# A transformer block on one core: the opening of the attention stage put in another order

## The chip, the core and the metric

The kernel runs on one core of a Trainium2 chip. Its engines are TensorE (PE, matrix products; PEld is its loading of the stationary operand), VectorE (DVE), ScalarE (ACT), GpSimd (POOL) and SyncE (SP, which mostly issues transfers). Each engine works through its own list of instructions strictly in order, and semaphores hold an instruction back until what it reads is there. Operands lie in SBUF, products are accumulated in PSUM, and both are laid out as 128 partitions by so many columns. The metric is the device time of one execution in microseconds (us); lower is better. Before the change the median of three runs is 546.14 us (545.97 to 547.85).

## The reference

The block has a linear attention half (A) and a token-mixing MLP half (B), 2048 tokens by 1024 channels, weights and inputs in bf16:

```python
h  = x + A(layernorm(x), wqkv, wo)
h2 = h + B(layernorm(h), w1, b1, w2, b2)

# A, 32 heads of 32 channels
q, k, v = split(x @ wqkv)
phi = lambda t: where(t > 0, t + 1, exp(t)) + 1e-6
pq, pk = phi(q), phi(k)
kv  = einsum("bhsd,bhse->bhde", pk, v);  z = einsum("bhsd->bhd", pk)
o   = einsum("bhqd,bhde->bhqe", pq, kv) / (einsum("bhqd,bhd->bhq", pq, z)[..., None] + 1e-6)
A   = o @ wo

# B, over the token axis, after a layernorm of its own
u = gelu(einsum("bsd,sf->bdf", layernorm(x), w1) + b1)
B = transpose(einsum("bdf,fs->bds", u, w2) + b2)
```

`A_x` is [1, 2048, 1024], `A_wqkv` [1024, 3072], `w1` [2048, 3584], `w2` [3584, 2048].

## The kernel before

The 2048 tokens are cut into 16 tiles of 128 (`x_sb`, one row of 1024 channels per partition). Each tile is normalised: `bn_stats` over each half of 512 columns and `bn_aggr` on DVE give mean and variance (`ln_chunks`, L1098 and L1101), two small ACT instructions turn the variance into 1/sqrt (Ln, then Exp; L1104 and L1105; below "the scales"), and DVE subtracts and multiplies (L1108, `xn`). The result is turned so that channels lie on partitions (`xnT`): for tiles 0 to 3 by PE transposes into PSUM (`transpose_half`, L1444) and copies back by ACT (L1454, L1484, L1487), for later tiles by a transposing DMA issued by SP (L1125).

From `xnT` PE makes keys, values and queries. For tiles 0 and 1 this is done plainly, in units of 128 tokens by 512 output columns and eight matmuls, one for each block of 128 channels (`proj_mm`, L1129): `k_unit(i, c)` for the keys of tile i and column half c, `proj_unit(i, 2 + c)` for the values. Each matmul reads a slice of the weights `wkv`, which SP loads column half by column half: c = 0 in three pieces, c = 1 in two pieces of four channel blocks (L1428), c = 2 and 3 (the values) in one piece each (L1432), then the query weights `wq_sb`. The loads of the token tiles stand between them in the same queue: tile 2 ahead of the first piece of c = 1, tile 3 ahead of its second, tiles 4 and 5 behind the first half of `wq_sb`. Tile 0 comes as two halves of columns, one by SP and one by ACT's queue, and tile 1 by ACT's queue (`load_x`). While nothing has landed, PE does products on a tile of zeros (`warm_up`).

From tile 2 on, keys, values and queries are made in `Run`s of two tiles by the seven products of the Strassen-Winograd scheme. Each run's seven products `p1` to `p7` need sums of the weight blocks (`w_sums`, L1187: four for the keys, then four for the values) and of the token blocks (`x_sums`, L1202), all made by DVE. `run_step(n, prev)` interleaves a run with the last two products of the run before: `p1` of n, `p3` and `p4` of prev, then `p6`, `p2`, `p5`, `p7` of n. `p7` and `p3` end with a DVE addition (`add`, L1307 for keys and queries, L1284 for values) that reads PSUM, and `p4` writes on into the bank that the addition of `p7` has read, so PE's `p4` waits for that addition. The order of the runs is K(1), V(1), K(2), V(2), ..., with query runs between the later ones and three (r1, r2, r3) behind; the digit is the pair of tiles.

The feature map `phi` is made in parts (`phi_parts`): `act` writes exp into `e_sb` (L200) and, unless `lean`, relu into `r_sb` (L202), both on ACT; `dve` clips and shifts `e_sb` in place (L205, below "clip") and adds the two (L209, or L207 when lean; below "join"). A key or query run makes four such maps, named by token half and column half: `dve11`, `dve21`, `dve12`, `dve22`. In `run_step` `dve22` follows `p3`, and `dve21` follows `p6`; on DVE nothing lies between them, so the order there is clip, join, clip, join.

`pin` keeps the instructions it is given in program order on their engine; `ln_stats(i)` is the statistics of tile i, `ln_finish(i)` its scales, normalisation and transposing DMA. In the main loop (L1620 to L1698) `after6`, `after5`, `finish` and `after7` say behind which product of which run these stand. The four `k_unit`s, the transposes of tiles 2 and 3 and their DVE and ACT work stand in the order written out by hand at L1490 to L1545. Two `memset`s of `zz` (L1681, L1682), which need nothing, are placed by the scheduler between DVE's first statistics. The MLP half after 183 us is not touched.

Of the kernel before, what the change touches and what calls it, by code (L numbers as in the profile page):

```python
# [10 lines left out]
P = 128  # L11
# [26 lines left out]
def kernel(  # L38
# [156 lines left out]
    def phi_parts(dst, src, n, pool, view=lambda t: t, lean=False):  # L195
        e_sb = pool.tile([P, n], BF16, tag="phi_e", name="e_sb")
        r_sb = None if lean else pool.tile([P, n], BF16, tag="phi_r", name="r_sb")

        def act():
            pin(nc.scalar.activation(e_sb[:], src, ACT.Exp))  # L200
            if not lean:
                pin(nc.scalar.activation(r_sb[:], src, ACT.Relu))  # L202

        def dve():
            pin(nc.vector.tensor_scalar(e_sb[:], e_sb[:], 1.0, PHI_EPS, ALU.min, ALU.add))  # L205
            if lean:
                pin(nc.vector.scalar_tensor_tensor(dst, view(src), 0.0, view(e_sb[:]), ALU.max, ALU.add))  # L207
            else:
                pin(nc.vector.tensor_tensor(dst, view(e_sb[:]), view(r_sb[:]), ALU.add))  # L209

        return act, dve

    def phi_evac(dst, src, n, pool):
        for part in phi_parts(dst, src, n, pool):
            part()

    sactx = ctx.enter_context(ExitStack())
    mctx = ctx.enter_context(ExitStack())
# [792 lines left out]
    with ExitStack() as actx:  # L1011
# [33 lines left out]
        with ExitStack() as a1:  # L1045
# [5 lines left out]
            vaugs = [a1w.tile([P, ND * HB, DH + 1], BF16, name=f"vaug{t}") for t in range(NVA)]  # L1051
            for t in range(NVA):
                nc.vector.memset(vaugs[t][:, :, DH:DH + 1], 1.0)

            def heads(t, c):
                return t[:, c * JB * HB:(c + 1) * JB * HB, 0:DH]
# [22 lines left out]
            def load_x(i, halves=False, q=nc.sync):  # L1079
                x_sb = xload.tile([P, D], BF16, name="x_sb")  # L1080
                if halves:
                    nc.sync.dma_start(x_sb[:, 0:CW], x[i * P:(i + 1) * P, 0:CW])
                    pin(nc.scalar.dma_start(x_sb[:, CW:D], x[i * P:(i + 1) * P, CW:D]))
                else:
                    dma = q.dma_start(x_sb[:], x[i * P:(i + 1) * P, :])
                    if q is not nc.sync:
                        pin(dma)
                return x_sb
# [115 lines left out]
            class Run:  # L1204
# [56 lines left out]
                def dve11(self):  # L1261
                    pass

                def dve21(self):
                    pass

                def dve12(self):
                    pass

                def dve22(self):  # L1270
                    pass

            class VRun(Run):
                def __init__(self, q):
# [13 lines left out]
            class KRun(Run):  # L1288
# [25 lines left out]
                    self.phi[1, 1][0]()  # L1314

                def dve11(self):
                    self.phi[0, 0][1]()

                def dve21(self):
                    self.phi[1, 0][1]()  # L1320

                def dve12(self):
                    self.phi[0, 1][1]()

                def dve22(self):
                    self.phi[1, 1][1]()

            class QRun(KRun):
                lean = True
# [51 lines left out]
            def run_step(n, prev, after6=None, after5=None, after7=None, fill=None, after3=None):  # L1381
                if n is not None:
                    n.p1()
                else:
                    fill()
                prev.late22()
                prev.p3()
                if after3 is not None:
                    after3()
                prev.dve22()  # L1390
                prev.p4()
                if n is not None:
                    n.p6()
                prev.dve21()
                if after6 is not None:
                    after6()
                if n is not None:
                    n.p2()
                    n.p5()
                prev.late12()  # L1400
                if n is not None:
                    n.dve11()
                behind = QRun in (type(n), type(prev)) or type(n) is VRun
                if not behind:
# [24 lines left out]
                if k0 == 0:  # L1429
                    xs[3] = load_x(3)  # L1430
            for c in range(2, 2 * NDC):
                nc.sync.dma_start(wkv[:, :, c * CW:(c + 1) * CW], wqkv_v[:, :, D + c * CW:D + (c + 1) * CW])  # L1432
            for c in range(NDC):
                nc.sync.dma_start(wq_sb[:, :, c * CW:(c + 1) * CW], wqkv_v[:, :, c * CW:(c + 1) * CW])
                if c == 0:
# [11 lines left out]
            def stats(i):  # L1447
                for op in ln[i][3]():
                    pin(op)
# [21 lines left out]
                    phis[key][0]()  # L1471

            def phi_dve(*keys):
                for key in keys:
                    phis[key][1]()

            def k_unit(i, c):
                phis[i, c] = k_parts(i, c)
# [18 lines left out]
            stats(0)  # L1497
            pin(ln[1][1](0))
            norm_halves(0)
            transpose_first(0, 0, 0)  # L1500
            pin(ln[1][1](1))
            pin(ln[1][2]())
            stats(1)
            k_parts(0, 0, range(0, 6))
            norm_halves(1)
            transpose_first(1, 6, ND)
            ln_stats(2)
            stats(2)
            k_unit(1, 0)
            norm_halves(2)  # L1510
            phi_act((0, 0))
            k_unit(0, 1)
            phi_act((1, 0))
            transpose_in(2)
            ln_stats(3)
            stats(3)
            phi_dve((0, 0))
            w_sums(kmov, slice(0, 1))
            norm_halves(3)
            phi_dve((1, 0))  # L1520
            phi_act((0, 1))
            k_unit(1, 1)
            transpose_in(3)
            phi_dve((0, 1))
            x_sums(1)
# [93 lines left out]
            for q in range(1, NVP):  # L1619
# [6 lines left out]
                for n in runs:  # L1626
                    kind = type(n).__name__[0]
                    i = {"K": 2 * q + 3, "V": 2 * q + 4}.get(kind, NS)
                    if q == 5 and kind == "Q":
                        i = NS - 1 if n.half == 1 else NS  # L1630
                    elif q == 6 and kind == "K":
                        i = NS

                    def after6():
                        if i < NS:
                            ln_stats(i)

                    def after5():
                        if kind == "K" and q % 2 == 1:
                            kv_block(q - 2)  # L1640
                        if kind != "V" and (kind, q) != ("K", 2):
                            finish()

                    def finish():
                        if i < NS:
                            ln_finish(i)
                            load_next(i + 2)

                    def after7():
                        if (kind, q) == ("K", 2):  # L1650
                            finish()
                        if kind == "V":
                            if q != 5 and q + 1 < NVP:
                                x_sums(q + 1, slice(0, 2))
                            prev.dve12()
                            finish()
                            if q != 5 and q + 1 < NVP:
                                x_sums(q + 1, slice(2, 4))
                        if q == 5 and kind == "Q" and n.half == 1:
                            x_sums(q + 1, slice(0, 3))  # L1660
                        if kind == "K" and q in q_sums:
                            w_sums(qmov, q_sums[q])
                        for m, a in moved_at.get((kind, q, getattr(n, "half", 0)), ()):
                            q_moved(m, a)
                        for x in late_sums.get((kind, q), ()):
                            x_sums(x[0], x[1], late_parts)
                        if (kind, q, getattr(n, "half", 0)) in fill_at:
                            q_fill()
                        if n is runs[-1] and q == 7:
                            kv_accum(NS - 2)  # L1670
                            kv_accum(NS - 1)

                    def after3():
                        if q == 6 and type(prev) is QRun:
                            x_sums(q, slice(3, 4))

                    run_step(n, prev, after6, after5, after7, after3=after3)
                    prev = n
            first_parts, first_home = sums_home(NSC - 1)
            r1, r2, r3 = (QRun(u, half, home, late_mov) for u, half, home in ((1, 0, late_home), (1, 1, late_home), (0, 1, first_home)))  # L1680
            nc.vector.memset(zz[:, :, 0:3 * HB], 0.0)  # L1681
            nc.vector.memset(zz[:, :, 3 * HB:], float(S))  # L1682

            turned = kvbd[:].rearrange("p (b a) (r e) -> p a b r e", b=HB, e=DH)
            sums_v = kv_ps[:, :, 0:DH].rearrange("p (b a) e -> p a b e", b=HB)
# [147 lines left out]
        with ExitStack() as a3:  # L1833
# [137 lines left out]
            fill[1]()  # L1971
# [3 lines left out]
            r3.dve21()  # L1975
            last[1][0]()
            for f in (r3.dve22, r3.dve12, last[0][1], last[1][1]):
                f()
# [315 lines left out]
```

## Time and profile before

| | |
|---|---|
| median of the runs | 546.14 us (545.97, 546.14, 547.85) |
| profiled execution | 545.59 us, its span 543.7 us |
| PE busy | 538.0 us (99%) |
| DVE busy | 471.3 us (87%) |
| ACT busy | 315.2 us (58%) |
| chain that ended last | PE 95%, DMA 2%, ACT 1%, DVE 1% |
| first transposes on PE | 6.21 us |
| first product of K(1) on PE | 23.48 us |

The span is the time from the first to the last instruction of one execution as the profiler recorded it; 1.9 us of that execution's device time lies around it. A row of the timeline gives start, length, engine, line, operation, tiles, shapes and count, and in brackets the engine's idle time just before and what ended it. PE's matmuls overlap, so its true pace is read from the starts: sixteen matmuls of 512 columns in a row take 3.45 us in the chain of waits, 0.216 us each.

### The profile page before, as it was taken

To read this page: it belongs to the slowest core of one execution; us is meant where nothing else is said; L and a number is where in the kernel's file an instruction comes from. 1 tells how busy PE (TensorE), PEld (TensorE's weight loads), DVE (VectorE), ACT (ScalarE), POOL (GpSimd) and SP (SyncE) were. 2 spreads that over 40 slices of the span, in tenths; PEclk is the share of its full clock that TensorE was granted. 3 is DMA by queue.
4 is the path that set the end of the run, shared out by engine and by line. 5 is a ranking of instruction groups with operands and counts; after the bars stand their busy time and mean duration, and the time that the engine had idled before them with its cause. 6 is when DMAs were issued, how large, how long until landed. Compare 5 with 4: busy or idle time off the path is not lost.

```text
span 543.7 us, 10593 instructions
## 1 busy us (share of the span) xinstructions
PE 538.0 (99%) x4046; PEld 339.4 (62%) x4058; DVE 471.3 (87%) x934; ACT 315.2 (58%) x672; POOL 73.1 (13%) x78
## 2 busy tenths in 40 slices
PE   8999999999999999999999999999999999999997
PEld 3444456656874444456777777776455667867865
DVE  7999897867798678899999989999898899979877
ACT  5678778767787788666667677675210413312320
POOL 1000000000002450021123112120002103103111
PEclk9999999999999999999999999999999999999999
DMA  8944321203339999137375856756697759399344
GB/s 293 326 79 98 88 69 21 40 1 93 82 94 238 220 277 320 74 40 155 40 151 65 160 83 127 156 68 147 173 299 196 208 133 243 53 304 223 80 128 74
DMA packets 105378, 77.76 MB, mean 143 GB/s; under 512 B 16482, under 2 KB 97904, under 8 KB 105328
## 3 DMA queue, kind: packets, MB, share of 16 engines
q1 hardware_dynamic: 85536, 64.32, 42.3%
q0 software_dynamic: 19360, 12.34, 17.4%
q8 instruction: 31, 0.51, 0.4%
q10 hardware_dynamic: 432, 0.44, 0.2%
q14 instruction: 19, 0.16, 0.1%
HBM read 62.27 MB, written 11.67 MB: 136 GB/s over the span
## 4 chain that ended last, share of the span: by engine, by line
PE 95%; DMA 2%; ACT 1%; DVE 1%; issue 0%; SPq 0%; DVEq 0%
PE psI L253 32%; PE psC L253 20%; PE psA L253 5%; PE psB L253 5%; PE psC L1213 5%; PE acc_t L253 4%; PE psB L1213 4%; PE psA L1213 4%; PE psE L1213 2%; PE psC L1347 2%; PE psA L1347 2%; PE psB L1347 2%; PE psF L253 2%; DMA wkv<-in_A_wqkv_dram 2%; PE acc_t L1129 1%; PE psE L253 1%
## 5 line engine op out<-in xcount | busy, mean ns | idle before, releaser
L253 PEld LDWEIGHTS <-is 128*128 128x128 f16 x900 | 87.9, 98 | 32.5 <-issue 0.3
L253 PEld LDWEIGHTS <-wq 128*128 128x128 bf16 (+1 forms) x694 | 67.9, 98 | 36.7
L253 PEld LDWEIGHTS <-sa 128*128 128x128 f16 x467 | 45.6, 98 | 13.9 <-issue 1.0
L253 PEld LDWEIGHTS <-pqT 128*128 128x128 bf16 x256 | 24.7, 98 | 30.6 <-issue 1.3
L526 POOL DMA_DIRECT2D out_dram<-wq x28 | 24.3, 937 | 143.4 <-ACT wq L529 96.8
L253 PE MATMUL psC<-gs,wq 128*128 128x512 f16 x168 | 40.8, 379 | 0.0
L1894 POOL DMA_DIRECT2D h_bf<-in_A_x_dram x18 | 16.1, 1079 | 183.2 <-ACT h_bf L253 182.9
L1213 PEld LDWEIGHTS <-xs 128*128 128x128 f16 x224 | 21.6, 98 | 24.3 <-DVE xs L1202 0.3
L253 PE MATMUL psI<-hi,is 128*128 128x256 f16 x240 | 36.0, 272 | 0.0
L253 PE MATMUL psC<-hT,wq 128*128 128x512 f16 x112 | 34.1, 379 | 0.0
L253 PE MATMUL psC<-hT,sa 128*128 128x512 f16 x112 | 32.0, 379 | 0.0
L253 ACT COPY psI<-psI 128x256 f32<-128x256 f32 x60 | 21.5, 358 | 15.8 <-PE psI L253 13.4
L1213 PE MATMUL psA<-wkv,xnT 128*128 128x512 bf16 x104 | 27.8, 379 | 0.4
L1213 PEld LDWEIGHTS <-xnT 128*128 128x128 bf16 x168 | 16.3, 98 | 19.0 <-issue 0.2
L253 PE MATMUL psI<-gi,is 128*128 128x256 f16 x210 | 27.8, 273 | 0.0
L168 POOL DMA_DIRECT2D wq<-in_B_w_dram x12 | 15.4, 1284 | 89.4 <-ACT wq L253 43.3
L253 DVE TENSOR_TENSOR t<-psI,t 128x256 f32<-128x256 f32 (+1 forms) x45 | 20.4, 473 | 6.3 <-PE psI L253 5.0
L253 DVE TENSOR_TENSOR is<-wq 128x512 f16<-128x512 bf16 (+3 forms) x48 | 22.0, 458 | 0.0
L205 DVE TENSOR_SCALAR e_sb<-e_sb 128x512 bf16<-128x512 bf16 x64 | 18.1, 283 | 3.7 <-ACT e_sb L200 3.5
L1098 DVE BATCH_NORM_STATS2 st<-x_sb 128x6 f32<-128x512 bf16 x32 | 20.6, 682 | 0.9 <-DMA x_sb<-in_A_x_dram 0.9
L168 POOL DMA_DIRECT2D sa<-in_B_w_dram x12 | 15.4, 1308 | 42.7 <-ACT sa L253 32.5
L253 PE MATMUL acc_t<-wo_sb,pqT 128*128 128x512 f16 x88 | 20.0, 379 | 0.0
(307 smaller groups left out, 1263.7 us busy)
## 6 DMA issues: line engine op xcount, KB each, us to landing
wq<-in_B_w_dram SPq DMA_DIRECT2D x20, 448.0 KB, 6.1
gs<-parked SPq DMA_DIRECT2D x9, 896.0 KB, 4.9
wq<-in_B_w_dram SPq DMA_DIRECT2D x11, 512.0 KB, 4.7
wq<-in_B_w_dram SPq DMA_DIRECT2D x5, 1024.0 KB, 7.3
shared_sb<-rd_dram SPq DMA_DIRECT2D x32, 128.0 KB, 5.1
out_dram<-h_bf SPq DMA_DIRECT2D x16, 256.0 KB, 5.2
x_sb<-in_A_x_dram SPq DMA_DIRECT2D x14, 256.0 KB, 3.4
w2o<-in_B_w_dram SPq DMA_DIRECT2D x4, 896.0 KB, 9.6
```

The lines of the kernel that those rows point to most:

```text
L168: pin(nc.gpsimd.dma_start(t[:, ks, :], a21[:, ks, :], accum_op=ALU.add))
L205: pin(nc.vector.tensor_scalar(e_sb[:], e_sb[:], 1.0, PHI_EPS, ALU.min, ALU.add))
L253: return (lambda *a, **kw: pin(op(*a, **kw))) if self.always or getattr(Held, self.key) else op
L526: nc.gpsimd.dma_start(to, ot[:, a:b], accum_op=ALU.add)
L1098: return nc.vector.bn_stats(st[:, c, :], x_sb[:, c * CW:(c + 1) * CW])
L1129: mm = nc.tensor.matmul(pp[:, 0:CW], lhsT=xnT[:, kt, i * P:(i + 1) * P], rhs=wkv[:, kt, c * CW:(c + 1) * CW], start=(kt == 0), stop=(kt == ...
L1213: pin(nc.tensor.matmul(ps[:], lhsT=lhs[:, k, :], rhs=rhs[:, k, :], start=(start and k == 0), stop=(k == hk2 - 1), skip_group_check=True,))
L1347: pin(nc.tensor.matmul(out[:, j], lhsT=rhs[:, k, 2 * self.half + j, :], rhs=lhs[:, k], start=(start and j == 0 and k == 0), stop=(k == hk2 ...
L1894: pin(nc.gpsimd.dma_start(h_bfs[i][:, cols], x[rows(i), cols], accum_op=ALU.add))
```

## The change

It has six parts, all in the attention half.

1. Tile 0 is loaded in four pieces of 64 partitions by 512 columns, two from SP's queue and two from ACT's, in place of two pieces of 128 partitions by 512 columns.
2. Tile 0's second half goes from PSUM to `xnT` by DVE in place of ACT. ACT then makes the scales of tile 1 right behind its two copies of the first half.
3. The statistics of tile 3 stand ahead of the normalisation of tile 2 on DVE, and its scales ahead of the copies of tile 2 on ACT.
4. The key units of column half 1 are cut in two: first the four lower channel blocks of tile 0 and of tile 1, then the transposes of tile 2, then the four upper blocks of both. The loads of the value weights are cut in two the same way.
5. Feature maps are made in pairs on DVE, clip, clip, join, join (`phi_join`), in the opening and in every `run_step` (`dve2`, behind `p6`).
6. In V(1) the statistics of tile 6 move from behind `p6` to `finish` (behind the first two `x_sums` of pair 2), and its `ln_finish` moves into K(2). The `memset`s of `zz` go to the front.

On PE the number and shapes of instructions stay the same; DVE gets one copy more. The core of the diff:

```diff
-        def dve():
+        def clip():
             pin(nc.vector.tensor_scalar(e_sb[:], e_sb[:], 1.0, PHI_EPS, ALU.min, ALU.add))
+
+        def join():
             if lean:
                 pin(nc.vector.scalar_tensor_tensor(dst, view(src), 0.0, view(e_sb[:]), ALU.max, ALU.add))
...
+    def phi_join(*parts):
+        for step in range(2):
+            for _, dve in parts:
+                dve[step]()
...
                 if halves:
-                    nc.sync.dma_start(x_sb[:, 0:CW], x[i * P:(i + 1) * P, 0:CW])
-                    pin(nc.scalar.dma_start(x_sb[:, CW:D], x[i * P:(i + 1) * P, CW:D]))
+                    for c in range(NDC):
+                        cols = slice(c * CW, (c + 1) * CW)
+                        nc.sync.dma_start(x_sb[0:P // 2, cols], x[i * P:i * P + P // 2, cols])
+                        pin(nc.scalar.dma_start(x_sb[P // 2:P, cols], x[i * P + P // 2:(i + 1) * P, cols]))
...
+                def dve2(self):
+                    phi_join(self.phi[1, 1], self.phi[1, 0])
...
                 prev.p3()
...
-                prev.dve22()
                 prev.p4()
                 if n is not None:
                     n.p6()
-                prev.dve21()
+                prev.dve2()
...
             for c in range(2, 2 * NDC):
-                nc.sync.dma_start(wkv[:, :, c * CW:(c + 1) * CW], wqkv_v[:, :, D + c * CW:D + (c + 1) * CW])
+                for k0 in (0, hk):
+                    nc.sync.dma_start(wkv[:, k0:k0 + hk, c * CW:(c + 1) * CW], wqkv_v[:, k0:k0 + hk, D + c * CW:D + (c + 1) * CW])
...
-            transpose_first(0, 0, 0)
+            dst, tp = transpose_half(0, 0)
+            for k in range(0, hk, 2):
+                pin(nc.scalar.copy(dst[:, k:k + 2, :], tp[:, k:k + 2, :]))
+            dst, tp = transpose_half(0, 1)
             pin(ln[1][1](1))
             pin(ln[1][2]())
             stats(1)
+            pin(nc.vector.tensor_copy(dst, tp))
             k_parts(0, 0, range(0, 6))
             norm_halves(1)
             transpose_first(1, 6, ND)
             ln_stats(2)
             stats(2)
             k_unit(1, 0)
+            ln[3] = ln_chunks(3, xs.pop(3))
+            for c in range(NDC):
+                pin(ln[3][1](c))
             norm_halves(2)
+            pin(ln[3][2]())
             phi_act((0, 0))
-            k_unit(0, 1)
+            k_parts(0, 1, lo_k)
             phi_act((1, 0))
+            stats(3)
+            k_parts(1, 1, lo_k)
             transpose_in(2)
-            ln_stats(3)
-            stats(3)
-            phi_dve((0, 0))
+            phi_dve((0, 0), (1, 0))
+            phis[0, 1] = k_parts(0, 1, hi_k)
+            norm_halves(3)
             w_sums(kmov, slice(0, 1))
-            norm_halves(3)
-            phi_dve((1, 0))
             phi_act((0, 1))
-            k_unit(1, 1)
+            phis[1, 1] = k_parts(1, 1, hi_k)
             transpose_in(3)
...
                     def after6():
-                        if i < NS:
+                        if (kind, q) == ("K", 2):
+                            ln_finish(i - 1)
+                        if i < NS and (kind, q) != ("V", 1):
                             ln_stats(i)
...
                         if i < NS:
-                            ln_finish(i)
+                            if (kind, q) == ("V", 1):
+                                ln_stats(i)
+                            else:
+                                ln_finish(i)
                             load_next(i + 2)
```

More of the change, by code (lines that the diff above doesn't have):

```diff
@@ L209, in dve @@
                 pin(nc.vector.tensor_tensor(dst, view(e_sb[:]), view(r_sb[:]), ALU.add))
-        return act, dve
+        return act, (clip, join)
+    def phi_join(*parts):
+        for step in range(2):
+            for _, dve in parts:
+                dve[step]()
     def phi_evac(dst, src, n, pool):
-        for part in phi_parts(dst, src, n, pool):
-            part()
+        part = phi_parts(dst, src, n, pool)
+        part[0]()
+        phi_join(part)
     sactx = ctx.enter_context(ExitStack())
@@ L1053 @@
                 nc.vector.memset(vaugs[t][:, :, DH:DH + 1], 1.0)
+            nc.vector.memset(zz[:, :, 0:3 * HB], 0.0)
+            nc.vector.memset(zz[:, :, 3 * HB:], float(S))
             def heads(t, c):
@@ L1262, in dve11 @@
                     pass
-                def dve21(self):
+                def dve2(self):
                     pass
                 def dve12(self):
-                    pass
-                def dve22(self):
                     pass
@@ L1316, in dve11, with dve2 @@
                 def dve11(self):
-                    self.phi[0, 0][1]()
-                def dve21(self):
-                    self.phi[1, 0][1]()
+                    phi_join(self.phi[0, 0])
+                def dve2(self):
+                    phi_join(self.phi[1, 1], self.phi[1, 0])
                 def dve12(self):
-                    self.phi[0, 1][1]()
-                def dve22(self):
-                    self.phi[1, 1][1]()
+                    phi_join(self.phi[0, 1])
             class QRun(KRun):
@@ L1473, in phi_dve @@
             def phi_dve(*keys):
-                for key in keys:
-                    phis[key][1]()
+                phi_join(*(phis[key] for key in keys))
             def k_unit(i, c):
@@ L1970 @@
             out_mm(0, (0,))
-            fill[1]()
+            phi_join(fill)
             fold(3, [den_tile(), bank("f"), den_tile(), bank("e")])
@@ L1974 @@
             r3.late12()
-            r3.dve21()
             last[1][0]()
-            for f in (r3.dve22, r3.dve12, last[0][1], last[1][1]):
-                f()
+            r3.dve2()
+            r3.dve12()
+            phi_join(*last)
             xctx.close()
```

2 lines of the change are left out of this document (removed).

## The prediction

> **What bounds the kernel now.** I read the page's shares of busy time first, then its chain of waits, then that chain in order of time over the first 60 us, and last the engines' timelines around each place that the change touches.
>
> ```profile
> PE 538.0 (99%) x4046; PEld 339.4 (62%) x4058; DVE 471.3 (87%) x934; ACT 315.2 (58%) x672; POOL 73.1 (13%) x78
> ...
> PE 95%; DMA 2%; ACT 1%; DVE 1%; issue 0%; SPq 0%; DVEq 0%
> ```
>
> PE is the bound nearly everywhere, so only time in which PE waits can be won. The chain in order of time (start, length, what) shows such time in the opening alone:
>
> ```profile
> 0.75 3.02 DMA x_sb<-in_A_x_dram
> ...
> 4.28 8.16 DMA wkv<-in_A_wqkv_dram
> 12.48 1.02 PE acc_t L1129 x4
> ...
> 15.30 0.42 DVE xn L1108
> 15.77 0.72 PE tp L1444 x8
> 16.49 3.45 PE acc_t L1129 x16
> ```
>
> Matmuls in a row start 0.216 us apart (3.45/16). From PE's starts in the trace, its waits from 6.2 us to the values at 16.33: 0.31 for the first copy of tile 0; 0.16 at the fifth key product (free at 7.95, starts 8.11), for the upper weights of column half 0, which land at 8.06; 0.17 before tile 1's transposes (8.54 to 8.71), for its normalisation; 0.29 (12.19 to 12.48) for the upper weights of column half 1, landing at 12.43; 0.26 + 0.09 around tile 3's transposes at 15.77, for its normalisation. That is 1.28 us. From 24 to 183 us I find three more waits: 0.04 at 38.06, 0.06 at 146.2, 0.25 at 153.5. DVE stands behind all three, and it sets what can be won:
>
> ```profile
> 8.24 0.73 DVE L1108 TENSOR_SCALAR xn<-x_sb,mvx_all,rstd 128x512 bf16<-128x512 bf16 x2 [0.89 <-ACT rstd L1105]
> ...
> 22.95 1.28 DVE L1098 BATCH_NORM_STATS2 st<-x_sb 128x6 f32<-128x512 bf16 x2
> ...
> 37.36 0.65 DVE L1284 TENSOR_TENSOR vaug<-psC,e 128x512 bf16<-128x512 f32 x1
> ```
>
> ```profile
> 140.25 0.28 DVE L205 TENSOR_SCALAR e_sb<-e_sb 128x512 bf16<-128x512 bf16 x1
> 140.56 0.69 DVE L207 SCALAR_TENSOR_TENSOR pqT<-kt,e_sb 128x512 bf16<-128x512 f32 x1
> 141.17 0.29 DVE L205 TENSOR_SCALAR e_sb<-e_sb 128x512 bf16<-128x512 bf16 x1
> 141.63 0.43 DVE L209 TENSOR_TENSOR pqT<-e_sb,r_sb 128x512 bf16<-128x512 bf16 x1 [0.17 <-ACT r_sb L202]
> ```
>
> The second fence is DVE in step r1. The share of the transfer engines in half microseconds, behind the engines' busy times, says when the loads run at full rate:
>
> ```profile
> 1.50:2.00 0.50, 0.50 (x2) 0.15 (x1) 0.29 (x4) 0.33 (x1) 0.50 (x1) 1.00 0.23 37
> 2.00:2.50 0.50, 0.50 (x3) 0.20 (x2) 0.41 (x3) 0.50 (x1) 0.42 (x3) 1.00 0.39 109
> 2.50:3.00 0.50, 0.50 (x3) 0.23 (x2) 0.25 (x1) 0.46 (x1) 0.40 (x1) 1.00 1.04 352
> ```
>
> From 2.5 us on about 350 GB/s flow without a break to the loads' end, so each landing is set by the bytes ahead of it in the queue.
>
> **The change, part by part.**
>
> *Tile 0 in four pieces.* Each queue issues one load more, at 0.40 us (SP) and 0.41 (ACT); all that stands behind, tile 1 on ACT's queue and every weight on SP's, is issued 0.4 later. By 2.5 us 73 KB of the 256 of tile 0 have moved (37 and 109 GB/s for 0.5 us each), so 183 KB, 0.52 us of work, are left, enough to 3.0. Before, the first bytes flow about 0.5 us after the first issue ends (1.14); the next loads' issue now ends at 2.05, so they flow from about 2.6. The stream has no hole. Bounds of the delay d of all landings: 0 and 0.42. I take 0. An earlier column half of tile 0 gains nothing: its normalisation stands on DVE behind the first statistics of tile 1, which start at 5.13 while tile 1 lands at 5.11, and the fifth key product waits for weights until 8.06 anyway.
>
> *Second half copied by DVE, scales ahead.* The copy reads 512 columns of PSUM; nearest rows: DVE's casts from PSUM (0.68 to 0.69), a clip in SBUF (0.24 to 0.29). I take 0.69: it starts at 7.26 when tile 1's statistics end, and lands at 7.95 where ACT's landed at 7.78, hidden by the weights of 8.06. Queued behind it on DVE is tile 1's normalisation. Its scales no longer wait for ACT's third copy (0.60): they end at 7.86 instead of 8.20, the normalisation starts at 7.9 instead of 8.24, and PE's transposes can start at 8.37, before PE is free at 8.54. Gain 0.17.
>
> *Key units by halves, statistics of tile 3 first.* PE, 0.17 earlier, ends the unit of tile 1 at 11.16, does the two lower halves to 12.88 (weights in at 10.24), and needs tile 2 normalised. That now waits on DVE behind tile 3's statistics, and tile 3 lands at 10.94: statistics 10.97 to 12.18, normalisation from 12.2 by halves of 0.33, transposable 0.47 after each start: 12.67 and 13.0, PE needing them at 12.88 and 13.10. The margin is 0.1. The upper weights (12.43) are then long in: gain 0.29. DVE goes on with the aggregate, the pair of maps (1.2) and tile 3's normalisation at 14.2, transposable at 14.7 and 15.0 where PE comes at 15.06. Gain 0.35. The values start at 15.51 instead of 16.33, with their first weights in at 15.44 as before, or in part at 13.9 by the cut in two. Together 0.81.
>
> *What DVE gives back.* DVE reaches the statistics of tile 4 at 22.4: from 14.84 behind the normalisation, w_sum 1.14, map 0.73, 0.12 for ACT's copies, x_sums 1.46, w_sum 1.14, map 0.73, two w_sums 2.27. But tile 4 lands only at 22.91 (issued 12.73, 10.2 to landing), where DVE just met it before. So from 22.95 on DVE stands where it stood, against a PE 0.81 earlier. To the addition that `p4` of K(2) waits for, started at 43.30, DVE has the same work in another order; it loses 0.26 of waits (26.9 to 27.4) and one pair's saving. That saving s: in the rows above a clip is followed after 0.32 to 0.39 by its own join, while an instruction that needs nothing of the one before starts 0.08 before its end (0.43 join, next at 0.34). A pair thus saves about 0.3; bounds 0 and 0.33. The addition starts at 42.74, ends 43.43, and PE, which started `p4` at 44.10 and would come at 43.25, waits 0.23. The 0.04 at 38.06 goes, since tile 6's statistics (1.42 on DVE) no longer stand ahead of V(1)'s addition (37.36); `ln_finish` of tile 6 with its transposing DMA on SP comes about 1.5 us later, for K(3) at about 55, margin over 8. To here: -0.81 - 0.04 + 0.23.
>
> *The pairs further on.* In the other steps PE has 0.5 to 0.8 us of slack behind the addition, or DVE does no pair before it. In r2 the pair comes early enough (second exponent ready at 147.9, pair at 149.2): the 0.25 at 153.5 goes. In r1 it costs: the second exponent ends at 141.11, so the second clip starts at 141.13 as before, and the first join (0.61), done until now in the wait from 140.56, comes behind it; the step's DVE work ends at 142.28 instead of 141.97. `p4` has no slack there (0.06 of wait already): +0.31.
>
> The page *VectorE: DVE Perf Modes* of the Trainium skill, section "The DRAIN you can't avoid", says otherwise on s: the next operation does not start until the pipe is empty, with or without a semaphore, so reordering saves nothing. The rows disagree with that (0.34 after a join of 0.43).
>
> **Sum.** -0.81 - 0.04 + 0.23 + 0.31 - 0.25 = -0.56 us. The profiled execution goes from 545.59 to 545.03; it lies 0.55 under the median shown, and against that the time is 545.6.
>
> **The rivals.**
>
> *Nothing is given back.* If tile 4 lands earlier or r1's pair finds its exponent ready, -0.23 and -0.31 stay won: -0.81 - 0.04 - 0.06 - 0.25 = -1.16, 545.0. Against it: the landing and the exponent's end are both in the trace.
>
> *Pairs save nothing.* With s = 0 DVE starts the addition of K(2) at 43.04 and PE waits 0.53; r1 costs 0.43; r2 keeps its wait: -0.81 - 0.04 + 0.53 + 0.43 = +0.11, 546.2. It is the sum under the rule of the page named above. Against it: the rows of the joins.
>
> *Slower: the first tile lands late.* If the second piece on each queue pays its start again, tile 1 and all weights come later by d, nothing else hides it, and the sum is -0.56 + d. It decides from d = 0.56. With twice the issue time, 0.84, it is +0.28, 546.4. For it: the two loads on ACT's queue landed 1.3 us apart, and x_sb of tile 1 arrived without a moment to spare. Against it: the 183 KB still queued at 2.5 us.
>
> **How the numbers follow.** Chances: the forecast (545.1 to 546.0, d up to 0.4 in it) 0.56; nothing given back 0.14; pairs save nothing 0.12; first tile late 0.14; anything else 0.04. The predicted time is 545.6, the range 544.8 to 546.6: from a little under the best case to a little over the worst. Half a per cent, about what a measurement here can tell from no change, is 2.7 us; all PE waits that the change can reach add up to 1.6. So faster by more 0.03, within it 0.93, slower by more 0.04.
>
> **What would show it.** Right: values start on PE near 15.5, PE waits of 0.2 before `p4` of K(2) and 0.3 more in r1, none at 153. DVE idle before tile 4's statistics shows the landing. Wrong: the first statistics of tile 1 after 5.3, tile 2's transposes waiting past 13.1, or clip to clip in a pair taking 0.3 us or more.

## The result, and where the time went

The changed kernel takes 548.83 us (median of 15 runs, 546.3 to 550.98) against 546.61 us of the kernel before in the same rounds (15 runs, 545.76 to 548.65): a ratio of 1.0034, with an interval of 1.0018 to 1.0049. It is slower by about a third of a per cent. That lies within the half per cent that the prediction called no change, but the sign is wrong, and 548.83 is outside the range of 544.8 to 546.6. The profiled execution took 548.69 us with a span of 546.6; that is 3.10 us more than the profiled execution of before (545.59).

The page of the changed kernel, busy times and the shares of the chain that ended last:

```profile
PE 538.9 (99%) x4046; PEld 340.2 (62%) x4058; DVE 470.0 (86%) x935; ACT 314.8 (58%) x671; POOL 73.0 (13%) x78
...
PE 94%; DVE 2%; DMA 2%; issue 1%; ACT 1%; ACTq 0%; DVEq 0%; SPq 0%
```

The shares say nothing: PE is at 99% as before. The chain in order of time (start, length, what; ACTq is ACT's queue issuing a load) says where the time is:

```profile
0.74 0.57 ACTq L1095
...
1.35 0.88 ACTq L1095
...
2.26 4.71 DMA x_sb<-in_A_x_dram
6.99 0.03 DVE st L1110
7.03 0.58 issue
7.60 0.41 DVE xn L1120
...
8.06 0.41 PE tp L1452 x4
...
8.92 2.71 PE acc_t L1141 x6
...
19.02 3.45 PE acc_t L1141 x16
...
46.49 0.69 DVE kt L1317
...
47.23 1.02 PE psC L1225 x4
```

Before, the chain began with the landing of tile 0 and went on with weights. Now it begins with the two pieces of tile 0 on ACT's queue, and through them with tile 1, which is issued at 2.26 in place of 1.19 and lands at 6.97 in place of 5.11. Six products take 2.71 us where sixteen take 3.45. The values start 2.53 later (19.02 here, 16.49 in the row of before).

Three views explain these rows. The first is DVE in the opening:

```profile
6.99 0.70 DVE L1110 BATCH_NORM_STATS2 st<-x_sb 128x6 f32<-128x512 bf16 x1 [1.68 <-DMA x_sb<-in_A_x_dram]
7.60 0.72 DVE L1120 TENSOR_SCALAR xn<-x_sb,mvx_all,rstd 128x512 bf16<-128x512 bf16 x2
...
9.09 0.37 DVE L1514 COPY xnT<-tp 128x512 bf16<-128x512 bf16 x1
```

DVE has the statistics of tile 0 long done, and waits 1.68 us for tile 1, because the first statistics of tile 1 stand ahead of tile 0's normalisation. So a late tile 1 holds back tile 0 as well: PE's first transposes start at 8.06, 1.85 later than before. These are the issue of tile 1 and the same two steps of DVE in the kernel before, where tile 1 came in time:

```profile
1.19 0.46 ACTq L1085 DMA_DIRECT2D x_sb<-in_A_x_dram  x1
...
5.13 0.69 DVE L1098 BATCH_NORM_STATS2 st<-x_sb 128x6 f32<-128x512 bf16 x1
5.74 0.73 DVE L1108 TENSOR_SCALAR xn<-x_sb,mvx_all,rstd 128x512 bf16<-128x512 bf16 x2
```

The second is the transfers in half microseconds, the last two columns being the share of the transfer engines and the rate in GB/s:

```profile
2.00:2.50 0.50, 0.50 (x3) 0.20 (x2) 0.40 (x4) 0.00 (x0) 0.42 (x3) 1.00 0.46 150
2.50:3.00 0.50, 0.50 (x3) 0.23 (x2) 0.48 (x1) 0.10 (x1) 0.40 (x1) 1.00 0.59 180
3.00:3.50 0.50, 0.50 (x3) 0.03 (x1) 0.23 (x2) 0.50 (x1) 0.00 (x0) 1.00 1.18 162
3.50:4.00 0.50, 0.50 (x3) 0.13 (x1) 0.47 (x1) 0.50 (x1) 0.00 (x0) 1.00 0.70 98
4.00:4.50 0.50, 0.50 (x3) 0.13 (x2) 0.12 (x1) 0.18 (x1) 0.00 (x0) 1.00 0.94 260
```

The last three of these windows before the change:

```profile
3.00:3.50 0.50, 0.50 (x3) 0.03 (x1) 0.00 (x0) 0.00 (x0) 0.00 (x0) 1.00 1.07 307
3.50:4.00 0.50, 0.50 (x3) 0.13 (x1) 0.40 (x1) 0.00 (x0) 0.00 (x0) 1.00 1.05 395
4.00:4.50 0.50, 0.50 (x3) 0.13 (x2) 0.50 (x2) 0.00 (x0) 0.00 (x0) 1.00 1.03 376
```

Before, the rates from 1.5 to 4.5 us were 37, 109, 352, 307, 395 and 376, which makes 788 KB; here they are 0, 150, 180, 162, 98 and 260, which makes 425 KB. The 363 KB that are missing take 1.04 us at 350 GB/s, and everything behind is late by about that much: tile 3 lands at 12.04 (10.94 before), the upper weights of column half 1 at 13.54 (12.43 before).

The third is the same view further on, where the column before the transfers' is the granted TensorE clock:

```profile
9.00:10.00 1.00, 1.00 (x3) 0.32 (x4) 0.69 (x3) 0.64 (x3) 0.00 (x0) 0.50 1.10 370
10.00:11.00 1.00, 1.00 (x3) 0.29 (x2) 1.00 (x3) 0.00 (x0) 0.00 (x0) 0.50 1.06 368
11.00:12.00 1.00, 1.00 (x7) 0.72 (x6) 0.91 (x3) 0.00 (x0) 0.00 (x0) 0.50 1.09 349
```

PE had no work for 2.05 us ahead of the transposes, and then ran at half its clock until 12.4: products 0.427 apart in place of 0.216. From the starts of PE's instructions, that stretch costs about 1.7 us. A busy PE in these rows is not PE at its pace.

The opening thus adds up: 1.85 for the transposes, some 1.7 for the clock, less 0.97 of waits that were there before and are gone (0.16 + 0.17 + 0.29 + 0.26 + 0.09), is 2.6 against 2.53 measured. Past the opening PE waits 0.62 before `p4` of K(2), 0.31 more than before in r1, 0.04 less in V(1) and 0.25 less in r2: 0.64 more, 3.17 in all. At the end of the attention half PE is 3.18 behind. The MLP half takes the same in both profiles (358.64 and 358.62 us), so PE wins nothing back there.

### The profile page after: what moved, and what is told of

Same layout as the page of the kernel before. It is cut to its first block, busy times and chain, and to the rows that moved or that the text cites. A ratio compares the mean times of both kernels' runs of the same rounds, so it can differ in the third digit from the quotient of the medians.

```text
span 546.6 us, 10593 instructions
## 1 busy us (share of the span) xinstructions
PE 538.9 (99%) x4046; PEld 340.2 (62%) x4058; DVE 470.0 (86%) x935; ACT 314.8 (58%) x671; POOL 73.0 (13%) x78
## 4 chain that ended last, share of the span: by engine, by line
PE 94%; DVE 2%; DMA 2%; issue 1%; ACT 1%; ACTq 0%; DVEq 0%; SPq 0%
PE psI L261 31%; PE psC L261 19%; PE psA L261 5%; PE psB L261 5%; PE acc_t L261 4%; PE psC L1225 4%; PE psB L1225 4%; PE psA L1225 4%; PE acc_t L1141 3%; PE psC L1355 2%; PE psE L1225 2%; PE psA L1355 2%; PE psB L1355 2%; PE psF L261 2%; PE psE L261 1%; PE psE L1355 1%
```

## The experiments

The theory from the two traces: the four pieces make tile 1 and the whole stream late, and PE pays for tile 1 twice, by waiting and by the halved clock, while the other five parts do about what was forecast. Its rivals: another part of the change is what costs, or the halved clock is an accident of one execution. Within the pieces, their shape and their number are two causes to be told apart. Line numbers in the profiles below shift by a few with each edit; the tile names do not.

**Tile 0 in two pieces again, all else as changed.**

```diff
-                    for c in range(NDC):
-                        cols = slice(c * CW, (c + 1) * CW)
-                        nc.sync.dma_start(x_sb[0:P // 2, cols], x[i * P:i * P + P // 2, cols])
-                        pin(nc.scalar.dma_start(x_sb[P // 2:P, cols], x[i * P + P // 2:(i + 1) * P, cols]))
+                    nc.sync.dma_start(x_sb[:, 0:CW], x[i * P:(i + 1) * P, 0:CW])
+                    pin(nc.scalar.dma_start(x_sb[:, CW:D], x[i * P:(i + 1) * P, CW:D]))
```

> The changed kernel with tile 0 loaded in two pieces again. Theory A (the four pieces make tile 1 land at 6.97 instead of 5.11; DVE's queue holds tile 0's normalisation behind tile 1's first statistics; PE stands still for 2 us and runs at half clock until 12.3): tile 1 lands near 5.1, the granted clock stays at 1.00, the values start near 15.6, and the time is 2.5 to 3.3 us under the changed kernel's, 0.2 to 0.8 us under the kernel before. Theory B (the new order of the opening and the pairs cost the time, the pieces little): the time stays within 1 us of the changed kernel's.

545.69 us (11 runs) against 546.08 (21 runs), ratio 0.9995 (0.9986 to 1.0005). Tile 1 lands at 5.32, the first transposes start at 6.41, the clock is 1.00 throughout. The values start 0.76 earlier than before. Then it is given back, on DVE and then PE:

```profile
35.77 0.69 DVE L1292 TENSOR_TENSOR vaug<-psC,e 128x512 bf16<-128x512 f32 x1 [0.60 <-PE psC L1223]
...
43.14 0.68 DVE L1315 TENSOR_TENSOR kt<-psC,e 128x512 f32<-128x512 f32 x1
```

```profile
43.88 1.02 PE L1223 MATMUL psC<-pqT,xnT 128*128 128x512 f16 x4 [0.44 <-DVE kt L1315]
```

The last row is `p4` of K(2) (by PE's starts the wait is 0.61; the bracket counts from a modelled end). Against before, PE is 0.76 ahead in the opening, 0.23 at 53 us, 0.08 behind at 151 us and 0.16 ahead at 160 us. What is left of the other five parts together is too little for the timed runs to tell from nothing.

**The four pieces alone**, put into the kernel before (the edit above the other way round).

> The kernel before with the four pieces alone. Theory A: tile 1 lands near 7, PE idle for about 2 us before the first transposes, granted clock 0.5 for about 3.4 us, 2.5 to 4 us slower than before. Theory B: within 1 us of before.

549.07 us (5 runs) against 546.08, ratio 1.0053 (1.0039 to 1.0067). Its profile has tile 1 landing at 7.83, PE without work for 2.88 us, and products 0.427 apart from 9.8 to 12.3. The pieces alone cost all that the change costs.

**Tile 0's normalisation ahead of the first statistics of tile 1.**

```diff
-            pin(ln[1][1](0))
             norm_halves(0)
+            pin(ln[1][1](0))
```

> The changed kernel, four pieces kept, but on DVE tile 0's normalisation stands ahead of tile 1's first statistics, so that it no longer waits for tile 1. Theory A: the first transposes start near 6.4 instead of 8.06, PE's longest idle stretch stays under 1.5 us, the clock stays at 1.00, and with the loads still about 1 us late the time is 1.2 to 2.2 us under the changed kernel's. If the late loads alone set the time (theory C: the halved clock and the late transposes are covered by the weights landing 1.1 us late), it is within 0.5 us of the changed kernel's.

546.61 us (11 runs) against 546.08, ratio 1.0012 (1.0003 to 1.0021). Tile 1 still lands late, at 6.86, but PE no longer waits for it:

```profile
6.26 0.72 PE L1452 MATMUL tp<-ident,xn 128*128 128x128 bf16 x8 [0.50 <-DVE xn L1120]
7.12 1.04 PE L1141 MATMUL acc_t<-wkv,xnT 128*128 128x512 bf16 x4
9.56 0.59 PE L1141 MATMUL acc_t<-wkv,xnT 128*128 128x512 bf16 x2 [1.41 <-DMA wkv<-in_A_wqkv_dram]
```

The products start 0.216 apart, PE's full pace (this trace holds no clock records, and a view shows 1.00 where there are none). The next late load is the bound: the upper weights of column half 0, landing at 9.52, 1.38 later than in the kernel with two pieces. So the late load costs in two ways: by tile 1, which holds back the transposes through DVE's order, and by the stream as a whole.

**Nine more zero-tile products ahead of the first transposes.**

```diff
-            warm_up(1, ln[0][6][:])
+            warm_up(10, ln[0][6][:])
```

> The changed kernel with nine more products on the tile of zeros behind tile 0's aggregate, which keep PE busy from 5.8 to about 7.9; nothing else differs, the first transposes still start at 8.06. Theory A: the granted clock stays at 1.00, eight products take 0.216 instead of 0.427 us, the values start 1.5 to 1.9 us earlier than in the changed kernel, and the time falls by 1.2 to 1.9 us. Theory C: the products then wait for weights and the time falls by less than 0.5 us.

In its profile PE is never idle for long, the products start 0.216 apart (this trace holds no clock records either), and the end of the opening comes 1.43 earlier than in the changed kernel; that execution took 547.39. The timed runs do not follow: 548.24 (5 runs) against 546.08, ratio 1.0048 (1.0035 to 1.0062). This was put to the test again beside the changed kernel, below.

**The statistics of tile 6 back behind `p6`, `ln_finish` back in V(1), with tile 0 in two pieces.**

```diff
-                        if (kind, q) == ("K", 2):
-                            ln_finish(i - 1)
-                        if i < NS and (kind, q) != ("V", 1):
+                        if i < NS:
                             ln_stats(i)
...
-                            if (kind, q) == ("V", 1):
-                                ln_stats(i)
-                            else:
-                                ln_finish(i)
+                            ln_finish(i)
```

> The changed kernel with tile 0 in two pieces, and part 6 undone for tile 6: its statistics behind p6 of V(1) and its normalisation in V(1) again. Theory D (DVE now idles 0.60 us ahead of V(1)'s addition and does the 1.4 us of statistics behind it, so it is late for K(2)): PE's wait before p4 of K(2), 0.61 with two pieces alone, falls under 0.1, a wait of at most 0.15 appears before p4 of V(1), and the time is 0.3 to 0.6 us under that kernel's 545.7. Theory E (DVE is late there because tile 4 lands at 22.9 whatever the order): the wait stays above 0.4.

545.4 us (10 runs) against 546.06 (35 runs), ratio 0.9985 (0.9975 to 0.9994). The idle time ahead of V(1)'s addition is gone, the addition of K(2) starts 0.66 earlier, and PE comes to `p4` without a wait:

```profile
36.55 0.65 DVE L1292 TENSOR_TENSOR vaug<-psC,e 128x512 bf16<-128x512 f32 x1
...
42.48 0.68 DVE L1315 TENSOR_TENSOR kt<-psC,e 128x512 f32<-128x512 f32 x1
```

```profile
43.54 1.03 PE L1223 MATMUL psC<-pqT,xnT 128*128 128x512 f16 x4
```

So the 0.61 was made by part 6 of the change, which took 1.4 us of work out of a gap in which DVE could do nothing else.

**r1 without its pair, with tile 0 in two pieces** (`run_step` of r1 calls `phi_join` twice, once for each map).

> The changed kernel with tile 0 in two pieces, and the pair of maps in step r1 alone put back to clip, join, clip, join. If the pair makes the first join wait for the second exponent there, PE's wait before p4 of r1 falls from 0.37 to 0.06 and the time by 0.3 us, all other waits staying; if the wait comes from something else in that step it stays at 0.37.

The wait in r1 falls from 0.37 to 0.06, as before the change. 545.75 us (10 runs), ratio 0.9992 (0.998 to 1.0003): the mechanism is there, and its 0.31 is too little for the timed runs to show. (Its profiled execution, 546.77, has a wait of 1.35 us at 499 us in the MLP half that no other profile has.)

**Both edits together, with tile 0 in two pieces.**

> Tile 0 in two pieces, tile 6's statistics back, r1 unpaired: the opening's order and the other pairs stay. Theory: the gains add up to 0.6 to 0.9 us under the two-piece kernel's 545.7, that is 544.8 to 545.1, 1.0 to 1.3 us under the kernel before, if half a microsecond can be told at all. Against it: PE's other waits move up and take it back, and the time stays at 545.5 or above.

545.17 us (12 runs, 544.49 to 546.85) against 546.06, ratio 0.9987 (0.9976 to 0.9997), with a profiled execution of 544.77. Of the waits past the opening and in the attention half only 0.06 in r1 is left. Its median is the lowest here, 0.07 above the top of what was expected; its ratio does not tell it from the kernel with the statistics of tile 6 back alone (0.9985).

**Tile 0 in two pieces of 64 partitions by 1024 columns**: as many loads as before the change, in the shape that the change uses.

```diff
-                    for c in range(NDC):
...
+                    nc.sync.dma_start(x_sb[0:P // 2, :], x[i * P:i * P + P // 2, :])
+                    pin(nc.scalar.dma_start(x_sb[P // 2:P, :], x[i * P + P // 2:(i + 1) * P, :]))
```

> The changed kernel with tile 0 in two pieces of 64 partitions by 1024 columns, one for each queue: as few issues as before, in the new shape. If the number of loads made them late, the issues take 0.40 us again, tile 1 lands near 5.1 and PE does not go to half clock: 545.5 to 546.0. If 64 partitions are what costs, the issues take 0.56 us or more and tile 1 lands at 5.5 or later.

546.59 us (10 runs), ratio 1.0008 (0.9998 to 1.0018). The issues take 0.57 to 0.58 us, and the load behind them on ACT's queue, tile 1 with all its partitions, takes 0.86; it is issued at 1.36 and lands at 6.40. The shape alone lengthens the issues, its own and the next. It also slows what follows: by 4.5 us 617 KB have moved, against 788 before the change, and tile 1 takes 5.04 from issue to landing.

**Tile 0 in four pieces of 128 partitions by 256 columns**: as many loads as the change has, in the shape of before.

```diff
-                        nc.sync.dma_start(x_sb[0:P // 2, cols], x[i * P:i * P + P // 2, cols])
-                        pin(nc.scalar.dma_start(x_sb[P // 2:P, cols], x[i * P + P // 2:(i + 1) * P, cols]))
+                        lo, mid, hi = c * CW, c * CW + CW // 2, (c + 1) * CW
+                        nc.sync.dma_start(x_sb[:, lo:mid], x[i * P:(i + 1) * P, lo:mid])
+                        pin(nc.scalar.dma_start(x_sb[:, mid:hi], x[i * P:(i + 1) * P, mid:hi]))
```

> Tile 0 in four pieces of 128 partitions by 256 columns: as many loads as in the changed kernel, but all partitions in each. Theory S (the shape of 64 partitions makes each issue long, 0.57 instead of 0.40, and the one behind it 0.88): the issues take about 0.40 each, tile 1 is issued near 1.6 us (0.74 + 2 x 0.41), lands near 5.5 to 5.7, the first transposes stand at 6.6 to 6.8, the clock stays at 1.00, and the time is about 546, within 0.4 of the kernel in two pieces. Theory C (the number of loads): the second issue on each queue takes 0.8 or more whatever its shape, tile 1 is issued past 2.0 and lands past 6.5, the clock falls to 0.50 behind the first transposes, and the time is 548 to 549.

547.46 us (10 runs) against 545.83 (17 runs), ratio 1.0024 (1.0011 to 1.0037). Neither theory stands whole. ACT's queue issues two pieces in 0.90 and tile 1 at 1.67, so the long issues do belong to the 64 partitions; but tile 1 lands at 6.42, as late as with the other shape:

```profile
0.74 0.90 ACTq L1095 DMA_DIRECT2D x_sb<-in_A_x_dram  x2
1.67 0.45 ACTq L1097 DMA_DIRECT2D x_sb<-in_A_x_dram  x1
```

```profile
2.50:3.00 0.50, 0.50 (x3) 0.23 (x2) 0.48 (x1) 0.50 (x1) 0.40 (x1) 1.00 1.40 258
3.00:3.50 0.50, 0.50 (x3) 0.03 (x1) 0.30 (x2) 0.44 (x1) 0.00 (x0) 1.00 0.31 37
3.50:4.00 0.50, 0.50 (x3) 0.13 (x1) 0.50 (x2) 0.00 (x0) 0.00 (x0) 1.00 0.29 76
```

There is a hole in the stream: for a microsecond the transfer engines are busy to a third and move 37 and 76 GB/s, between the small pieces and the large loads, though the issue of three large loads had begun by 2.2. So the pieces cost in two ways that add: later issues, and about 0.8 us more of flight (tile 1 takes 4.75 from issue to landing, 3.9 before). The flight is not a matter of size alone, since it was 5.04 behind two pieces of 64 partitions and 128 KB. What the stream waits for in that hole no view shows; it stays open. The profiled execution, 546.44, is among the shorter of the ten, and its clock is 1.00; four of the ten list a granted clock of 0.997.

**The changed kernel once more, and the one with more zero products once more, side by side.**

> The changed kernel once more, unchanged, for a second profiled execution. Theory H (the halved clock is what most executions pay): tile 1 lands between 6.8 and 7.8 us, the windows from 9 to 12.3 us show 0.50 again, and the time is 548 to 549.5. Rival (the halved clock was an accident of one execution): clock 1.00 in all windows and yet about 548.5, or a profile near 546.5.

> The changed kernel with nine more zero-tile products once more, beside the changed kernel in the same call. Theory H: clock 1.00 in every window, the values start near 17.6 against 19.0, and the median lies 1.2 to 1.6 under the changed kernel's of this call. Rival: the median lies within 0.6 of the changed kernel's, as it did before; then the later landing alone costs most of it in the timed runs, or the zero products give something back.

The changed kernel: 548.11 us (4 runs), ratio 1.0040 (1.0024 to 1.0056). Tile 1 lands at 6.67, the first transposes start at 7.76, and the clock is halved again, here from 7.7 to 11.1:

```profile
8.00:9.00 1.00, 0.96 (x9) 0.66 (x7) 0.97 (x4) 0.60 (x3) 0.00 (x0) 0.50 0.97 352
9.00:10.00 1.00, 1.00 (x3) 0.30 (x2) 0.74 (x3) 0.45 (x3) 0.00 (x0) 0.50 1.08 366
```

With more zero products: 547.85 us (8 runs), ratio 1.0031 (1.0020 to 1.0042); clock 1.00 everywhere, now from records. At the end of the attention half PE is 1.24 ahead of the run beside it, and at the end of the kernel 0.24. The MLP half took 359.9 us in place of 358.9, with waits of 0.47, 0.52 and 0.44 for DVE's additions:

```profile
PE psI L261 <- DVE e L261: 0.9, 3, 0.4
```

(The view of waits: who waits for whom, sum, times, longest, by modelled ends.) The profile of that kernel's first run has two waits at the same places (0.43 and 0.23). So without the halved clock the opening ends 1.4 and 1.2 earlier, shown twice and although the transposes stand 0.25 and 0.11 later behind the added products. But an opening that is that much earlier did not make the kernel faster by an amount that these runs can tell. Whether the MLP half gives such a lead back regularly, or only in these executions, is open; a single wait of 0 to 0.66 near 330 us differs from one profiled execution to the next in other kernels too.

The granted clocks of the timed runs do not settle it either. One stretch of 3.41 us at half clock in a span of 546.6 makes a mean of 0.997. Six of the changed kernel's first 15 executions list 0.996 or 0.997, three of these four, and four of the five with the pieces alone, so the halved clock is no accident of one execution. But the six have a median of 548.59 us, and the nine that list 1.0 one of 549.18. Since an execution without clock records lists 1.0 too, the nine need not have had the full clock. That the halved clock stretches the opening is shown in three profiles; what it adds to the timed runs is not shown.

## Why the prediction was wrong

The step that failed is **"Tile 0 in four pieces"**. It gave the delay d the bounds 0 and 0.42 and took 0, on the sentence "The stream has no hole". Three things were wrong in it:

- The price of an issue was taken from loads of 128 partitions (0.40, 0.41). The pieces have 64, and each takes 0.57, the second on ACT's queue 0.88. Tile 1 is issued 1.07 later, not 0.41.
- The stream has a hole. The 183 KB were to keep it full to 3.0; in fact it ran at 98 to 180 GB/s from 2.0 to 4.0, 425 KB had moved by 4.5 us against 788 before, and the later loads are 1.1 late.
- The bound did not follow the one load that had no margin. The step used DVE's order (the first statistics of tile 1 ahead of tile 0's normalisation) to show that an earlier half gains nothing, and the slower rival added that tile 1 arrives without a moment to spare. The same row says that every delay of tile 1 is a delay of the first product. Measured, tile 1 came 1.86 later and the transposes 1.85; with tile 0's normalisation put first they start at 6.26 although tile 1 is as late.

**The slower rival** had the right mechanism, at 0.14, with too small a price: d at 0.84 gave 546.4. It also assumed that PE loses only what it waits. The halved clock was in no term; with it the profiled opening comes out, though the timed runs do not show its price. The Trainium skill (*TensorE: Matmul & The Clock Gate*, Part 1 on the clock gate) states it: after an idle window of about 3.4 us the array gets half its clock, until it has been busy for about as long. The three stretches at 0.50 agree (3.41 us each); the idle time does not have to be 3.4, since 2.05 and 2.88 in one piece and 0.90 with 1.33 were enough, while in the profiles with 1.45 and 1.46 (the two halves by rows, the four pieces by columns) the clock stayed at 1.00.

The traces allow a closer reading. Their clock records begin and end on a grid of steps of 3.41 us, which starts elsewhere in each execution. By the modelled ends of its products, PE was busy for 1.40, 1.46 and 0.77 us of the step ahead of the three halved ones, and for 1.07 of the step ahead of a fourth, at the end of the kernel with tile 6's statistics back. Each step with 1.97 or more was followed by the full clock, in all eleven traces that have clock records. So what counts in these traces is how busy PE was within one step, with the border somewhere between 1.46 and 1.97, and the same gap can halve the clock in one execution and not in the next, as the listed clocks of the four pieces by columns suggest.

The Trainium skill also has a rule against the change itself that the prediction passed over. *DMA: Bandwidth & Descriptors*, "Rules for kernel authors", says of two transfers to disjoint partition halves not to bother, and that transfers under 64 KB are mostly overhead. The pieces are just 64 KB. The runs agree: with the other five parts the ratio is 1.0008 for halves of 64 partitions against 0.9995 for halves of 128, and the four pieces alone make it 1.0053.

The other steps can be read from the kernel with two pieces, where the stream is as assumed:

- **The opening's gain**: forecast 0.81, measured 0.76 in this profile. The three other kernels with this opening show 0.49, 0.75 and 0.42; in those with 0.49 and 0.42 the upper weights of column half 0 landed at 8.41 and 8.49, where the forecast had 8.06. The forecast is thus the upper end of what came. The waits it named went.
- **Second half copied by DVE**: taken 0.69 by the casts from PSUM, measured 0.37, nearer to the rows of the clip than to those of the casts. It was hidden either way.
- **"What DVE gives back"**: DVE's wait for tile 4 came as forecast (0.54). But "the same work in another order" missed the 0.60 us that DVE idles ahead of V(1)'s addition, since the work that had filled it was moved behind. The addition of K(2) started at 43.14, not 42.74, and PE waited 0.61, not 0.23. The text had even named the moved statistics, as a gain of 0.04. Moving them back brings K(2)'s wait to nothing.
- **The pair's saving s**: taken 0.3, bounds 0 and 0.33, measured 0.38, just outside. In the changed kernel the pair stands beside a single map:

```profile
36.98 0.49 DVE L205 TENSOR_SCALAR e_sb<-e_sb 128x512 bf16<-128x512 bf16 x2
37.38 0.76 DVE L211 TENSOR_TENSOR pk<-e_sb,r_sb 128x512 bf16<-128x512 bf16 x2
...
40.51 0.29 DVE L205 TENSOR_SCALAR e_sb<-e_sb 128x512 bf16<-128x512 bf16 x1
40.90 0.42 DVE L211 TENSOR_TENSOR pk<-e_sb,r_sb 128x512 bf16<-128x512 bf16 x1
41.24 1.28 DVE L1110 BATCH_NORM_STATS2 st<-x_sb 128x6 f32<-128x512 bf16 x2
```

A single map takes 0.73 from clip to the next instruction (40.51 to 41.24), two would take 1.46. The pair starts its clips 0.20 apart, its first join 0.20 behind the second clip, and its joins 0.34 apart: with 0.34 behind the last, 1.08. The rival in which pairs save nothing is out. Of the Trainium skill's page *VectorE: DVE Perf Modes*, "The DRAIN you can't avoid", the prediction gave one rule without the closing sentence of the same paragraph, which says that an operation that is not held starts earlier; the rows bear out that sentence.

- **The pair in r1**: forecast +0.31, measured 0.31, and r2's wait of 0.25 went. Both right. DVE in r1, where the second clip waits for its exponent and the first join stands behind it:

```profile
143.36 0.28 DVE L205 TENSOR_SCALAR e_sb<-e_sb 128x512 bf16<-128x512 bf16 x1
144.25 0.29 DVE L205 TENSOR_SCALAR e_sb<-e_sb 128x512 bf16<-128x512 bf16 x1 [0.61 <-ACT e_sb L200]
144.46 0.69 DVE L209 SCALAR_TENSOR_TENSOR pqT<-kt,e_sb 128x512 bf16<-128x512 f32 x1
```

With two pieces the sum is -0.76 - 0.04 + 0.61 + 0.31 - 0.25 = -0.13 (the trace has -0.16 at 160 us), against a forecast of -0.56: 0.38 of the gap is K(2). With four it is 2.53 - 0.04 + 0.62 + 0.31 - 0.25 = 3.17. Of the tests that the prediction named, "the first statistics of tile 1 after 5.3" was the right one: they start at 6.99.

## What to carry to other kernels

Ahead of a stream that the opening lives on, take the price of a load from a load of the same shape, and ask of a split first who stands behind it in the queue: the load with no margin pays. When a change moves work away from in front of a wait, look at whether the engine can use the time; DVE could not, and the work then stood before the next thing that mattered. In the profiled executions a TensorE idle for some two microseconds lost nearly as much again by the clock.

## What the runs showed of the hardware

- Issuing a first load of 64 partitions took 0.56 to 0.58 us on SP's and on ACT's queue, one of 128 partitions 0.39 to 0.41. The load issued behind one of 64 was slower too: 0.78 to 0.88 on ACT's queue, 0.57 to 0.58 on SP's; behind one of 128 it took 0.45 to 0.47 and 0.42 to 0.43.
- Four loads of 64 KB and 64 partitions in front cost the stream 1.04 us of full rate; with 128 partitions each there was still a hole of about a microsecond at 37 to 76 GB/s.
- The granted TensorE clock fell to 0.50 for one step of 3.41 us after a step in which PE had been busy for 0.77 to 1.46 us; after 1.97 or more it stayed full. The profile of before, with at least 2.22 in every step up to PE's last product, has no such stretch.
- A copy of 512 bf16 columns from PSUM took DVE 0.37 us; additions that read f32 from PSUM took 0.64 to 0.69.
